# W_o's first sixteen heads loaded by a four-engine and a sixteen-engine transfer instead of one, and W_down in six transfers instead of seven

## The chip, the cores and the metric

The kernel runs on one core of one Trainium2 chip. The metric is the device time of the program in microseconds (us). Times inside the program are counted from the start of the span of the one execution that the profiler recorded; engines are named as in the profile: PE multiplies matrices (PEld loads its weights), DVE, ACT and POOL work on vectors, SP issues nearly all transfers. The core has 16 transfer engines; below, "transfer engine" always means one of these.

## What is computed

One decode step of a transformer block: two sequences, one new token each, 512 features, 32 heads of 128, a cache of 8192 keys and values for each head.

```python
x = A_x
h = x + _A_ref(_layernorm(x, axis=-1), A_k_cache, A_v_cache, A_wq, A_wo)
h2 = h + _B_ref(_layernorm(h, axis=-1), B_W_gate, B_W_up, B_W_down)
# _A_ref: softmax(q k^T / sqrt(128)) v for every head, joined, times wo (4096 x 512)
# _B_ref: (relu(x W_gate) * (x W_up)) W_down, 1376 hidden features
```

Inputs are bfloat16. Keys and values are 268 MB of the 281 MB that the program reads; the weights are the rest, W_o 4.2 MB and W_gate, W_up and W_down 1.4 MB each.

## The kernel before

The work goes in steps of four heads of one sequence: 15 such steps (the last has number Q, L53) and then two half steps of two heads, p0 and p1. For a step the keys come as one transfer of 128 partitions and the values as another (`load_tile`, L160). DVE multiplies the keys by the query (L372) and adds up the products in halves (L390, L392), PE takes a share of the scores (L339, L348), ACT makes the exponentials (L412, L430), and PE multiplies the values by them (L443). Three buffers, `bufs[0..2]`, hold keys and values in turn, and the weights of the end of the program go into the parts that are free by then: W_o into the second half of `bufs[0]` (`wo`, L125), W_gate and W_up into `bufs[2]`, W_down into `bufs[1]`.

The schedule is written out by hand. SP issues transfers in program order, and an issue waits for whatever its buffer and its completion semaphore still hold. Eight completion semaphores go round, so a transfer is issued only when the transfer eight before it has landed whole. The transfers at the end, in order: keys of p0 and p1, values of p0, W_o's heads 0 to 15 (`load_set(0)`, L559), the values of p1 in four pieces (L564), W_o's heads 16 to 23, 24 to 27 and 28 to 29 (`load_set`, L566), heads 30 and 31 (L567), W_gate and W_up in two pieces each (L578), W_down in seven pieces (L583), the output (L675). W_down's pieces are the entries of `FSETS` (L73), pairs of first row and number of 128-row chunks; the last entry, 96 rows of which are new, is loaded and used first. A transfer of W_o lays n heads as n*512 consecutive elements on each partition: 16 KB a partition for heads 0 to 15, over 128 partitions.

After p1's softmax PE multiplies W_o by the heads' outputs (L496, L503), DVE adds the residual (L614) and makes the normalised vector `hn` (L621), PE runs W_gate and W_up (L634) and then W_down chunk by chunk (L664, in the order of the pieces), DVE adds the residual (L669), and PE and DVE turn the result for the store (L673, L674).

Of the kernel before, what the change touches and what calls it, by code (L numbers as in the profile page):

```python
# [13 lines left out]
def _free(t, offset, dims):  # L14

    return bass.AP(tensor=t.tensor, offset=t.offset + offset, ap=[t.ap[0]] + [list(d) for d in dims])


def _dram(t, offset, dims):
    return bass.AP(tensor=t.tensor, offset=t.offset + offset, ap=[list(d) for d in dims])  # L20
# [3 lines left out]
def kernel(  # L24
# [13 lines left out]
    nc = tc.nc  # L38
    P = nc.NUM_PARTITIONS
    B, Sq, D = A_x.shape  # L40
    _, Hkv, Sk, Dh = A_k_cache.shape
    Hq = A_wq.shape[1] // Dh
    F = B_W_gate.shape[1]
# [23 lines left out]

    SETS = [(0, 16, 0), (16, 8, 16), (24, 4, 24), (28, 2, 28)]
    HM = 30
    SROWS = [n for _, n, _ in SETS]  # L70


    FSETS = [(0, 3), (3 * P, 3), (6 * P, 1), (7 * P, 1), (8 * P, 1), (9 * P, 1), (F - P, 1)]  # L73
    FC = 11
    AGAIN = 32

# [34 lines left out]
    hm = consts.tile([P, FC, B], bf16)  # L111
    quot = {r: consts.tile([P, Dh // r], bf16, name=f"quot{r}") for r in SROWS}
    rest = {r: consts.tile([P, r], bf16, name=f"rest{r}") for r in SROWS}
    orow = [consts.tile([P, r, B], bf16, name=f"orow{k}") for k, r in enumerate(SROWS)]
    sel = consts.tile([B, B, P // 2], bf16)
# [9 lines left out]
    wo = bufs[0][:, HALF:TILE]  # L125
# [43 lines left out]
    def ln_cols(src, dst_bkc, pfx):  # L169

        m_ps = ps.tile([P, B, KC], f32, tag="mx")
        nc.tensor.matmul(out=m_ps, lhsT=mean_w, rhs=src, start=True, stop=True)
        mean = small.tile([P, B], f32, tag=pfx + "mean")
        nc.vector.tensor_reduce(out=mean, in_=m_ps, axis=AXIS.X, op=ALU.add)
        dev = small.tile([P, B, KC], f32, tag=pfx + "dev")
        nc.vector.tensor_tensor(out=dev, in0=src, in1=_free(mean, 0, [[1, B], [0, KC]]), op=ALU.subtract)
        sq = small.tile([P, B, KC], f32, tag=pfx + "sq")
        nc.vector.tensor_tensor(out=sq, in0=dev, in1=dev, op=ALU.mult)
        v_ps = ps.tile([P, B, KC], f32, tag="mx")
        nc.tensor.matmul(out=v_ps, lhsT=mean_w, rhs=sq, start=True, stop=True)  # L180
        rstd = small.tile([P, B], f32, tag=pfx + "rstd")
        nc.vector.tensor_reduce(out=rstd, in_=v_ps, axis=AXIS.X, op=ALU.add)
        nc.scalar.activation(out=rstd, in_=rstd, func=ACT.Sqrt, bias=eps_col, scale=1.0)
        nc.vector.reciprocal(out=rstd, in_=rstd)
        nc.vector.tensor_tensor(out=dst_bkc, in0=dev, in1=_free(rstd, 0, [[1, B], [0, KC]]), op=ALU.mult)

    with tc.manual_schedule():
# [11 lines left out]
            out=nscale, in_=nscale, compare_op=ALU.not_equal, fill=-SCALE,  # L199
# [5 lines left out]
            out=ident_f, in_=ident_f, compare_op=ALU.not_equal, fill=1.0,  # L205
# [4 lines left out]
            out=sel, in_=sel, compare_op=ALU.not_equal, fill=1.0,  # L210
# [8 lines left out]
            out=pick, in_=pick, compare_op=ALU.not_equal, fill=1.0,  # L219
# [20 lines left out]
        ln_cols(xc, xn.rearrange("p c b -> p b c"), "l1")  # L240
        for r in SROWS:
            nc.vector.tensor_reduce(out=rest[r], in_=_free(ident, 0, [[1, r], [r, P // r]]), axis=AXIS.X, op=ALU.max)
# [5 lines left out]
        for g0 in range(0, NQ, 4):  # L248
            for n0 in range(NH * g0 * Dh, NH * (g0 + 4) * Dh, 4 * Dh):
                q_ps = ps2.tile([B, 4 * Dh], f32, tag="o")  # L250
                for c in range(KC):
                    nc.tensor.matmul(  # L252
                        out=q_ps, lhsT=xn[:, c, :], rhs=wq_sb[:, c, n0:n0 + 4 * Dh], start=(c == 0), stop=(c == KC - 1),
                    )
                nc.vector.tensor_copy(qrow[:, n0:n0 + 4 * Dh], q_ps)  # L255
            for b in range(B):
                r_ps = ps2.tile([P, 4, Dh], f32, tag="tp")
                for j in range(NH):
                    nc.tensor.matmul(
                        out=r_ps[j * (P // NH):(j + 1) * (P // NH)], lhsT=sel[:, b, 0:P // NH],  # L260
# [5 lines left out]
        for j in range(2):  # L266
            nc.tensor.matmul(
                out=r_ps[j * (P // 2):(j + 1) * (P // 2)], lhsT=sel[:, B - 1, :],
# [215 lines left out]
        def lay_rows(k, sps):  # L484

            r = SROWS[k]
            or_ps = ps.tile([P, B, r], f32, tag="mx")
# [4 lines left out]
        def attend_set(k, r0=0, r1=None):  # L492
            for c0 in range(r0, SROWS[k] if r1 is None else r1):
                for c in range(KC):
                    at = (SETS[k][2] + c0) * D + c * P
                    nc.tensor.matmul(  # L496
                        out=att_ps[:, c, :], lhsT=wo[:, at:at + P], rhs=orow[k][:, c0, :],
                        start=(k == 0 and c0 == 0 and c == 0), stop=False, skip_group_check=True,
                    )

        def attend(h):
            for c in range(KC):
                nc.tensor.matmul(  # L503
                    out=att_ps[:, c, :], lhsT=wo[:, h * D + c * P:h * D + (c + 1) * P], rhs=ocol[:, h, :],
                    start=False, stop=(h == Hq - 1), skip_group_check=True,
                )
# [45 lines left out]
        own_sums(Q)  # L552
        def load_set(k):
            h0, n, at = SETS[k]
            nc.sync.dma_start(
                out=wo[:, at * D:(at + n) * D], in_=_dram(A_wo, h0 * Dh * D, [[n * D, P], [1, n * D]]),
            )

        load_set(0)  # L559
        products(p0, p0.na)  # L560

# [3 lines left out]
        for k in range(1, len(SETS)):  # L565
            load_set(k)  # L566
        nc.sync.dma_start(  # L567
            out=wo[:, HM * D:Hq * D].rearrange("p (h n) -> p h n", n=D),
            in_=_dram(A_wo, HM * Dh * D, [[D, P], [Dh * D, Hq - HM], [1, D]]),
        )  # L570
# [6 lines left out]
        for w, src, c, n in ((0, B_W_gate, 0, 2), (0, B_W_gate, 2, 2), (1, B_W_up, 0, 2), (1, B_W_up, 2, 2)):  # L577
            nc.sync.dma_start(  # L578
                out=wgu[:, w, c:c + n], in_=_dram(src, c * P * F, [[F, P], [P * F, n], [1, F]]),
            )  # L580
        for f0, n in FSETS[-1:] + FSETS[:-1]:
            fc = FC - 1 if f0 == F - P else f0 // P
# [5 lines left out]
            out=z2_ps, lhsT=ones, rhs=_free(zc, ((B - 1) * NQ + groups[Q][1]) * NH, [[1, nb]]), start=True, stop=True,  # L588
# [18 lines left out]
        for k in range(1, len(SETS)):  # L607
            attend_set(k)
        for h in range(HM, Hq):
            attend(h)  # L610
# [15 lines left out]

        chunks = [(f0 + c, n) for f0, n in FSETS for c in range(n)]
        UP = 6

        def through(w_ps, k, part, cs=range(KC)):  # L630
# [18 lines left out]
            out=gate, in0=g_ps, scalar=0.0, in1=_free(rvar, 0, [[0, FC], [1, B]]), op0=ALU.max, op1=ALU.mult,  # L649
# [12 lines left out]
        for fc in order:  # L662
            for c in range(KC):
                nc.tensor.matmul(  # L664
                    out=d_ps[:, c, :], lhsT=wd_sb[:, fc, c * P:(c + 1) * P], rhs=hm[:, fc, :],
# [40 lines left out]
```

## Time and profile before

| | us |
|---|---|
| median of three runs | 661.41 (661.36 to 661.43) |
| the profiled execution | 661.18 |
| its span, first to last instruction | 659.4 |
| DVE busy | 556.6 (84%) |
| PE busy | 349.5 (53%) |
| last piece of W_down landed, in the span | 656.21 |

Transfers ran at a mean of 427 GB/s, and queue 1, which SP feeds, kept the 16 transfer engines busy for 99.0% of the span. Two other queues, called "instruction", brought 16 packets of 16 KB and six of 8 KB. The page's second part shows the span in slices, its third the queues, its fourth the chain of work that ended last. Beside these the trace has one row for each packet (start, duration, size, queue) and the moment of each step of a completion semaphore. A transfer over 128 partitions shows 16 such steps, the store of eight partitions eight together and one ahead of them, and the load of two rows of x shows two packets of data. A step is taken here as one transfer engine's end of its share. The rows do not carry the number of the transfer engine.

### The profile page before, as it was taken

What the parts mean: (1) busy time and instruction counts of PE and PEld (TensorE: products, weight loads), DVE (VectorE), ACT (ScalarE), POOL (GpSimd) and SP (SyncE); (2) the same over time, 40 slices, a digit from 0 to 9 for tenths busy, and PEclk for the clock granted to TensorE, in tenths of its full rate; (3) what the DMA queues carried; (4) which work ended last, traced back from release to release, by engine and by line L of the source; (5) the groups of instructions that cost most, each with busy time, mean ns of one, the idle gap of its engine ahead of it and who ended that gap; (6) DMA issues with size and microseconds to landing.
All of it is one profiled execution on the core that took longest, in us unless ns stands there. A gap on an engine that the chain in (4) does not pass through costs nothing.

```text
span 659.4 us, 5114 instructions
## 1 busy us (share of the span) xinstructions
PE 349.5 (53%) x2107; PEld 157.9 (24%) x2107; DVE 556.6 (84%) x250; ACT 126.6 (19%) x367; POOL 5.3 (1%) x32
## 2 busy tenths in 40 slices
PE   3530924709175380916548192753809458191886
PEld 1210311304022130402214041221403224030346
DVE  2399697989979798897969889696997979999992
ACT  1130030301103030120302102030310304200780
POOL 3000000000000000000000000000000000000000
PEclk9875875959679595966959597785957869696975
DMA  9999999999999999999999999999999999999997
GB/s 382 445 442 445 402 430 437 445 446 434 402 441 434 441 438 417 437 429 438 441 430 425 433 426 441 441 422 441 418 442 434 430 433 433 430 421 430 423 410 273
DMA packets 8458, 281.40 MB, mean 427 GB/s; under 512 B 882, under 2 KB 1780, under 8 KB 3316
## 3 DMA queue, kind: packets, MB, share of 16 engines
q1 hardware_dynamic: 8432, 281.09, 99.0%
q8 instruction: 16, 0.26, 0.2%
q14 instruction: 6, 0.05, 0.0%
q10 hardware_dynamic: 4, 0.00, 0.0%
HBM read 281.09 MB, written 0.00 MB: 426 GB/s over the span
## 4 chain that ended last, share of the span: by engine, by line
DVE 44%; DMA 36%; PE 18%; ACT 1%; issue 1%; DVEq 0%; ACTq 0%; SPq 0%
DMA tile<-in_A_k_cache_dram 31%; DVE tile L372 20%; DVE tile L390 19%; PE pv_ps L443 16%; DVE scol L392 2%; DMA tile<-in_B_W_up_dram 2%; DMA tile<-in_A_wq_dram 2%; PE q_ps L252 1%; DMA tile<-in_B_W_down_dram 1%; DVE pgq L417 1%; ACT ecol L412 1%; DVE pm L396 1%; DVE qrep L392 0%; DVE pm L407 0%; DVE hmax L409 0%
## 5 line engine op out<-in xcount | busy, mean ns | idle before, releaser
L443 PE MATMUL pv_ps<-tile,pgq 128*16 128x512 bf16 x960 | 238.5, 415 | 205.6 <-DVE pgq L417 192.9
L372 DVE TENSOR_TENSOR tile<-tile,qrep 128x28672 bf16<-128x28672 bf16 (+3 forms) x16 | 230.2, 14391 | 50.9 <-DMA tile<-in_A_k_cache_dram 50.9
L390 DVE TENSOR_TENSOR tile<-tile 128x14336 bf16<-128x14336 bf16 (+5 forms) x68 | 235.2, 3459 | 2.3
L443 PEld LDWEIGHTS <-pgq 128*16 128x16 bf16 x960 | 91.3, 96 | 347.0 <-DVE pgq L417 203.4
L349 ACT ACTIVATE tile<-t_ps 128x1024 bf16<-128x1024 bf16 x53 | 52.6, 1022 | 18.1 <-PE t_ps L348 17.5
L448 ACT ACTIVATE pv<-pv_ps 16x512 f32<-16x512 f32 (+1 forms) x16 | 9.4, 588 | 242.9 <-PE pv_ps L443 242.8
L412 ACT ACTIVATE ecol<-scol,nmax 128x256 bf16<-128x256 f32 x14 | 7.1, 507 | 193.0 <-DVE nmax L411 193.0
L339 PE MATMUL row_ps<-tile,qz 128*32 128x512 bf16 (+1 forms) x106 | 32.4, 387 | 18.8 <-ACT tile L349 18.7
L348 PE MATMUL t_ps<-ident,tile 128*128 128x128 bf16 x424 | 31.5, 225 | 5.5 <-DMA tile<-in_A_k_cache_dram 5.5
L348 PEld LDWEIGHTS <-tile 128*128 128x128 bf16 x424 | 25.1, 101 | 20.6 <-issue 14.9
L392 DVE TENSOR_REDUCE scol<-tile 128x224 f32<-128x1792 bf16 (+1 forms) x14 | 28.7, 2048 | 0.5
L307 PE MATMUL z_ps<-zc,ones 128*128 128x16 f32 (+1 forms) x8 | 2.4, 375 | 42.7 <-DVE zc L298 42.4
L378 ACT ACTIVATE tile<-tile 128x128 bf16<-128x128 bf16 x80 | 23.4, 293 | 3.5 <-DVE tile L372 3.5
L417 DVE TENSOR_TENSOR pgq<-ecol,ownb 128x1024 bf16<-128x1024 bf16 x15 | 10.4, 691 | 10.3 <-ACT ecol L412 10.3
L372 DVE TENSOR_TENSOR tile<-tile,qpair 128x5120 bf16<-128x5120 bf16 (+1 forms) x4 | 17.7, 4417 | 0.0
L339 PEld LDWEIGHTS <-qz 128*32 128x32 bf16 (+1 forms) x106 | 8.6, 93 | 28.6 <-issue 22.7
L378 ACT ACTIVATION_READ_ACCUMULATOR tile<-tile 128x1 f32 x80 | 14.9, 186 | 0.0
L252 PE MATMUL q_ps<-tile,xn 128*2 128x512 bf16 x32 | 9.1, 447 | 8.4 <-DMA tile<-in_A_wq_dram 8.4
L255 DVE CAST tile<-q_ps 2x512 bf16<-2x512 f32 x8 | 5.4, 679 | 9.7 <-PE q_ps L252 9.7
L364 ACT ACTIVATE scol<-sc_ps 32x32 f32<-32x32 f32 (+1 forms) x56 | 11.9, 213 | 7.8 <-PE sc_ps L359 7.3
L307 PEld LDWEIGHTS z_ps<-zc,ones 128*128 128x128 f32 x8 | 2.0, 310 | 43.0 <-DVE zc L298 27.6
L359 PE MATMUL sc_ps<-ident_f,tile 32*128 32x32 f32 (+1 forms) x60 | 6.4, 224 | 11.0 <-ACT tile L356 11.0
(122 smaller groups left out, 129.3 us busy)
## 6 DMA issues: line engine op xcount, KB each, us to landing
tile<-in_A_k_cache_dram SPq DMA_DIRECT2D x2, 4096.0 KB, 23.4
tile<-in_A_wq_dram SPq DMA_DIRECT2D x1, 4096.0 KB, 12.2
tile<-in_A_v_cache_dram SPq DMA_DIRECT2D x1, 4096.0 KB, 20.5
tile<-in_A_v_cache_dram SPq DMA_DIRECT2D x4, 1024.0 KB, 22.7
tile<-in_A_wo_dram SPq DMA_DIRECT2D x1, 2048.0 KB, 25.0
tile<-in_B_W_gate_dram SPq DMA_DIRECT2D x2, 688.0 KB, 13.9
tile<-in_B_W_up_dram SPq DMA_DIRECT2D x2, 688.0 KB, 12.8
tile<-in_A_wo_dram SPq DMA_DIRECT2D x1, 1024.0 KB
```

The lines of the kernel that those rows point to most:

```text
L252: nc.tensor.matmul(out=q_ps, lhsT=xn[:, c, :], rhs=wq_sb[:, c, n0:n0 + 4 * Dh], start=(c == 0), stop=(c == KC - 1),)
L339: nc.tensor.matmul(out=row_ps, lhsT=z, rhs=s.kt[:, (nv + c0 + k) * Dh:(nv + c0 + k + 4) * Dh], start=(u == 0), stop=(u == U - 1),)
L348: nc.tensor.transpose(t_ps[:, k, :], s.kt[:, t * Dh:(t + 1) * Dh], ident)
L349: nc.scalar.activation(out=s.kt[:, (nv + c0) * Dh:(nv + c0 + TPC) * Dh], in_=t_ps.rearrange("p t s -> p (t s)"), func=ACT.Copy,)
L364: nc.scalar.activation(out=scols[s.i][r, nv:s.nt].rearrange("p (u t) -> p t u", t=4), in_=sc_ps[r, :, :, j], func=ACT.Copy,)
L372: nc.vector.tensor_tensor(out=kv, in0=kv, in1=_free(s.qr, 0, [[0, n], [1, Dh]]), op=ALU.mult)
L378: nc.scalar.activation(out=kv, in_=kv, func=ACT.Copy, accum_out=scols[s.i][:, t:t + 1])
L390: nc.vector.tensor_tensor(out=lo, in0=lo, in1=hi, op=ALU.add)
L392: nc.vector.tensor_reduce(out=scol[:, s.na:s.nv], in_=_free(s.kt, s.na * Dh, [[Dh, s.nv - s.na], [1, 8]]), axis=AXIS.X, op=ALU.add,)
L412: nc.scalar.activation(out=ecol, in_=scols[s.i], func=ACT.Exp, scale=SCALE, bias=nmax, accum_out=zs[:, s.b, s.g:s.g + 1],)
L417: nc.vector.tensor_tensor(out=s.pg, in0=_free(ecol, 0, [[VG, s.nt // VG], [0, NH], [1, VG]]), in1=_free(ownb, 0, [[0, s.nt // VG], [VG, NH ...
L443: nc.tensor.matmul(out=pv_ps[s.i][r, :], lhsT=s.pg[:, u].rearrange("p j t -> p (j t)"), rhs=s.vt[:, u * VG * Dh:(u + 1) * VG * Dh], start= ...
```

## The change

Heads 0 to 15 of W_o, 2 MB in one transfer over 128 partitions, become two transfers. The first takes partitions 0 to 15 and describes the source as four blocks of four rows, so that four transfer engines carry four rows of 16 KB each. The second takes partitions 16 to 127, seven rows for each of sixteen. W_down's pieces become (4, 3, 1, 1, 1 chunks and the last 128 rows) instead of (3, 3, 1, 1, 1, 1 and the last 128 rows). The count of transfers stays the same. No instruction of another engine changes.

```diff
+    P4 = 16
+    LEVEL = 1
-    FSETS = [(0, 3), (3 * P, 3), (6 * P, 1), (7 * P, 1), (8 * P, 1), (9 * P, 1), (F - P, 1)]
+    FSETS = [(0, 4), (4 * P, 3), (7 * P, 1), (8 * P, 1), (9 * P, 1), (F - P, 1)]
...
         def load_set(k):
             h0, n, at = SETS[k]
+            w = n * D
+            if k < LEVEL:
+                nc.sync.dma_start(
+                    out=wo[0:P4, at * D:(at + n) * D],
+                    in_=_dram(A_wo, h0 * Dh * D, [[P4 // 4 * w, 4], [w, P4 // 4], [1, w]]),
+                )
+            r0 = P4 if k < LEVEL else 0
             nc.sync.dma_start(
-                out=wo[:, at * D:(at + n) * D], in_=_dram(A_wo, h0 * Dh * D, [[n * D, P], [1, n * D]]),
+                out=wo[r0:P, at * D:(at + n) * D], in_=_dram(A_wo, h0 * Dh * D + r0 * w, [[w, P - r0], [1, w]]),
             )
```

## The prediction

> **What bounds the kernel now.** I read the page first: its busy slices, its queues and its chain.
>
> ```profile
> DMA  9999999999999999999999999999999999999997
> ...
> DMA packets 8458, 281.40 MB, mean 427 GB/s; under 512 B 882, under 2 KB 1780, under 8 KB 3316
> ...
> q1 hardware_dynamic: 8432, 281.09, 99.0%
> q8 instruction: 16, 0.26, 0.2%
> q14 instruction: 6, 0.05, 0.0%
> ```
>
> The transfer engines are never idle until the last slice; queue 1 alone fills 99.0% of them. So the time is set by when the bytes have arrived plus what must follow the last byte. DVE's 44% of the chain is work under whose cover transfers run. The end of the chain in order of time says what follows:
>
> ```profile
> 638.03 12.80 DMA tile<-in_B_W_up_dram
> 650.86 0.03 issue
> 650.89 5.32 DMA tile<-in_B_W_down_dram
> 656.21 0.05 issue
> 656.26 0.28 PE d_ps L664 x4
> 656.56 0.18 DVE y L669
> ```
>
> The last chunk of W_down lands at 656.21, its four matmuls follow, and 659.4 - 656.21 = 3.2 us of tail run after it. Third, the windows over the last stage (busy of PE, PEld, DVE, ACT, POOL; then clock, share of the 16 transfer engines, GB/s):
>
> ```profile
> 652.00:653.00 1.00, 0.48 (x8) 0.41 (x6) 0.00 (x0) 0.00 (x0) 0.00 (x0) 0.50 0.94 340
> 653.00:654.00 1.00, 1.00 (x35) 1.00 (x35) 0.61 (x4) 0.00 (x0) 0.00 (x0) 0.50 0.73 268
> 654.00:655.00 1.00, 0.74 (x29) 0.68 (x27) 0.47 (x4) 0.00 (x0) 0.00 (x0) 0.50 0.50 178
> 655.00:656.00 1.00, 0.93 (x32) 0.85 (x30) 0.00 (x0) 0.00 (x0) 0.00 (x0) 0.50 0.28 95
> ```
>
> The share falls from 0.94 to 0.28 over three us: the engines do not end together, and the last ones set the end. The steps of the completion semaphores give the spread. The first load's sixteen shares land within 0.56 us, the last W_down piece's within 3.28: five within 0.32 of the first (652.93), one at 0.82, three at 1.57 to 1.82, seven at 2.89 to 3.28. The mean is 1.79, so perfectly level shares would land 1.49 us (0.23%) earlier: a ceiling for levelling.
>
> Where the lag comes from is in the packet rows. On an engine each packet begins within a few ns of the one before, so a share can be followed. The 16 KB instruction packets fall on eight engines in turn, two rounds; the first makes its engine 1.4 us late (spread 0.53 before it, 1.95 after). The 8 KB ones cost others about 0.4 each. Five engines have met none. Eight that fetch, eight that do not: the change helps if the four engines of its first transfer are among the five.
>
> **The change, part by part.** *Shares.* 16 KB packets of queue 1 take 0.613 us. Before, each engine has eight rows in this load. After, twelve have seven: -0.61 us. Four have four and seven, eleven: +1.84.
>
> *W_down's pieces.* By the trace's packets an engine's share was 8 x (2 x 0.122 + 5 x 0.046) = 3.79 us and becomes 8 x (0.159 + 0.122 + 4 x 0.046) = 3.72, and one 9 ns marker goes: -0.08 for all. The extra transfer's marker costs the four 0.01. Sum: twelve engines -0.69, four +1.77.
>
> *The end, if the four are of the five.* The twelve end at 656.21 - 0.69 = 655.52; the four at no more than 653.25 + 1.77 = 655.02. So the last piece lands at 655.52. What is late next is PE: W_down's 44 matmuls begin at 654.69, after `hm` (L659), whose own chain waits on DVE and PE. W_up's 44, with the same shapes, took 1.33 us without a wait, so W_down's cannot end before 656.02. Before, they ended at 656.54. The larger first piece (four chunks) ends 32 KB into each share, at about 652.33 + 8 x 0.159 = 653.6 on the latest engine, before it is needed. So of the 0.69 saved, 656.54 - 656.02 = 0.52 reaches the end.
>
> *Waits and queues.* The number of transfers is the same; between W_o's first load and W_down's first piece each takes the next completion semaphore. One issue of 0.33 to 0.43 us is added on SP behind values of p0. The values of p1 come behind it, but they wait for PE's reads until 611.07 anyway, 5 us later. W_o's heads 24 to 27 would now wait for the values of p0 (625.63) instead of p1's keys (615.90). The earliest engine comes to them only at 639.6, when heads 16 to 23 are done, so that costs nothing. W_down's last piece waits for a transfer landed at 649.10, no longer 650.83. Cover of the weights moved: the old load landed at 630.52 and is first read at 638.53, 8 us.
>
> *Four engines: which?* The page has no row for such a transfer. The nearest are the load of x (two rows, two data packets) and the store (eight rows, eight steps together). They bear out that few rows use few engines, not which. A weak hint: the two engines whose first packet starts first (1.77) never fetch. Bounds: the four gain nothing in lag (all of the five) or are of the seven. I take the first, since only half the engines fetch and the early starters do not.
>
> The Trainium skill ("DMA: Bandwidth & Descriptors", "Why a DMA increments its semaphore by 16 and not by 1") says that the engine count is the largest up to 16 that divides both sides' outer dimension, and that they are the lowest-numbered. By it the first transfer takes engines 0 to 3 and the second all sixteen; the trace's two and eight agree on the count, and no row here shows a number.
>
> **Rivals.**
>
> *Late four* (0.17). If the four are of the seven, the last landing is 656.21 + 1.77 = 657.98 at worst and the sum +1.8: 663.2. If one is of the middle three, 653.25 - 0.32 + 1.82 + 1.77 = 656.52, +0.3: 661.7 (0.05, in effect no change). For it: eight of sixteen engines fetch. Against it: the hint above.
>
> *Shared destinations* (0.33), the slower side. In a load of 128 partitions each engine has eight of them for itself, in this kernel always the same. With seven rows each, the second transfer's rows fall across those bounds, and two engines can write into one engine's old partitions at once. If such a pair shares the rate that one had (32 KB packets never took under 1.211 us, 27 GB/s), seven packets of 0.613 = 4.29 us become up to 8.58. Then the last landing is between 656.21 - 0.69 + 2.15 = 657.67 (half of the packets in pairs) and 659.81 (all): +1.5 to +3.6, 662.9 to 665.0, middle 664.0. It decides from 0.69 / 4.29 = 16% of the time in pairs: below that a gain is left. For it: every load of the trace has 128 partitions, so the rate seen may be a destination's and not an engine's. Against it: an 8 KB instruction packet, which goes to no tile, took 0.309 us, the same 27 GB/s, so the engine alone has that limit.
>
> The Trainium skill has a rule here: "SBUF — State Buffer", "Door 1: The DMA port swizzle", gives each port eight partitions in groups of four and 27.2 GB/s, and measures 196 GB/s for 64 partitions. Under that rule, if each engine takes seven neighbouring rows, my estimate from that section's port table is +3 to +5 us. The trace's 27 GB/s agrees with the figure and cannot say whose limit it is.
>
> *The levelling does nothing*: the extra 48 KB could be too much for its four, or W_down's end could be bound by PE at once. That is the 661.7 case above; it shares its chance.
>
> **How the numbers follow.** Forecast: the profiled execution 661.18 - 0.52 = 660.66; the median is 0.23 above that execution, so 660.9. Its own range is 660.6 (the whole 0.69 comes through) to 661.3. Chances: level 0.43, no net change 0.07, late four 0.17, shared destinations 0.33. A measurement of this kernel can tell about 0.2% (1.3 us) from no change. The level case is 0.08% and lies within, with the no-change case: 0.50. For faster by 0.2% nearly all of the ceiling would have to come through, past the PE bound: 0.02, out of the level case, whose other 0.41 counts here as no change. Late four at 1.8 (0.27%) and shared destinations are slower: 0.50, of which 0.02 is a mild collision that stays within 0.2%: so 0.02, 0.50, 0.48. The range goes from 660.6 to 665.0, the far end of the last rival; about one in ten is left out above, and little below.
>
> **What would show it.** Level: after W_o's second load the spread of a load's sixteen steps falls from 3.3 us to about 2.6, the windows' share stays above 0.9 until 654 and drops within two us, and PE's W_down matmuls run without a gap from 654.7. Late four: the spread grows to about 5. Shared destinations: 16 KB packets of queue 1 well above 0.613 us, and loads behind them landing later on engines that fetch nothing. I am wrong altogether if the chain no longer ends in W_down's transfer or if instruction packets move to other engines.

## The result, and the profile after

The changed kernel takes 670.12 us (median of four runs, 669.16 to 671.23) against 661.38 of the kernel before: 1.0133 times as long, 95% interval 1.0121 to 1.0146, 8.7 us slower. The prediction was 660.9 with a range of 660.6 to 665.0. It was wrong, on the slower side. The profiled execution after took 669.16 us with a span of 667.4, 8.0 more than the span before; the readings below are of these two.

The chain still ends in W_down's last piece. Start, duration and step:

```profile
643.68 13.49 DMA tile<-in_B_W_gate_dram
657.21 0.03 issue
657.24 6.97 DMA tile<-in_B_W_down_dram
664.20 0.05 issue
664.25 0.28 PE d_ps L673 x4
664.55 0.18 DVE y L678
```

The last piece lands at 664.20 where it landed at 656.21, and the same 3.2 us of tail follow. So the 8.0 us are all in when the bytes arrive. Where the transfers lost them shows in the windows around W_o's first load; last two columns: share of the 16 transfer engines that is busy, and GB/s. Before:

```profile
620.00:625.00 5.00, 3.62 (x17) 1.41 (x15) 4.79 (x6) 2.80 (x17) 0.00 (x0) 1.00 0.94 401
625.00:630.00 5.00, 1.93 (x6) 0.97 (x7) 5.00 (x3) 2.94 (x17) 0.00 (x0) 0.77 0.99 419
630.00:635.00 5.00, 5.00 (x15) 1.49 (x13) 5.00 (x3) 5.00 (x36) 0.00 (x0) 0.54 1.01 419
635.00:640.00 5.00, 5.00 (x76) 2.76 (x75) 4.86 (x5) 4.98 (x35) 0.00 (x0) 1.00 1.02 423
```

After:

```profile
620.00:625.00 5.00, 5.00 (x25) 2.06 (x22) 4.79 (x6) 2.63 (x19) 0.00 (x0) 1.00 0.99 306
625.00:630.00 5.00, 1.78 (x7) 0.97 (x7) 5.00 (x3) 3.12 (x17) 0.00 (x0) 0.75 0.97 206
630.00:635.00 5.00, 5.00 (x15) 1.57 (x13) 5.00 (x3) 5.00 (x36) 0.00 (x0) 0.57 1.01 210
635.00:640.00 5.00, 4.67 (x58) 2.32 (x56) 4.86 (x5) 5.00 (x36) 0.00 (x0) 1.00 0.95 293
```

The share stays near 1.0 while the rate falls to half. A busy share says only that a packet is under way on each engine. Times 5 us, the four differences are 475, 1065, 1045 and 650 KB, together 3.2 MB; at 419 GB/s that is 7.7 us, nearly the whole loss.

The packet rows say the same. W_o's 128 packets of 16 KB took 1.20 us on average (0.63 to 1.67), against 0.614 before. The trace also shows which engines carried the first transfer: its completion semaphore makes sixteen late steps, 623.18 to 630.63, where a transfer on four engines would make four (the probe run below has such a transfer). The trace gives that transfer's destination as 16 rows of 16 KB. So it ran on sixteen engines, one row each, and with the second transfer's seven every engine had eight rows as before. No engine was relieved.

### The profile page after: what moved, and what is told of

Read it like the earlier page. It is cut to its first block, busy times and chain, and to the rows that moved or that the text cites. A ratio compares the mean times of both kernels' runs of the same rounds, so it can differ in the third digit from the quotient of the medians.

```text
span 667.4 us, 5115 instructions
## 1 busy us (share of the span) xinstructions
PE 356.2 (53%) x2107; PEld 160.4 (24%) x2107; DVE 556.6 (83%) x250; ACT 126.7 (19%) x367; POOL 5.4 (1%) x32
## 4 chain that ended last, share of the span: by engine, by line
DVE 41%; DMA 40%; PE 17%; ACT 1%; issue 1%; DVEq 0%; ACTq 0%; SPq 0%
DMA tile<-in_A_k_cache_dram 30%; DVE tile L374 18%; DVE tile L392 18%; PE pv_ps L445 16%; DMA tile<-in_A_v_cache_dram 4%; DVE scol L394 2%; DMA tile<-in_B_W_gate_dram 2%; DMA tile<-in_A_wq_dram 2%; PE q_ps L254 1%; DMA tile<-in_B_W_down_dram 1%; DVE pgq L419 1%; ACT ecol L414 1%; DVE pm L398 1%; DVE qrep L394 0%; DVE pm L409 0%
## 5 line engine op out<-in xcount | busy, mean ns | idle before, releaser
L445 PE MATMUL pv_ps<-tile,pgq 128*16 128x512 bf16 x960 | 243.9, 422 | 201.2 <-DVE pgq L419 188.1
L361 PE MATMUL sc_ps<-ident_f,tile 32*128 32x32 f32 (+1 forms) x60 | 6.4, 224 | 11.1 <-ACT tile L358 11.1
## 6 DMA issues: line engine op xcount, KB each, us to landing
tile<-in_A_v_cache_dram SPq DMA_DIRECT2D x1, 4096.0 KB, 23.6
```

What stands on the lines that cost most here:

```text
L445: nc.tensor.matmul(out=pv_ps[s.i][r, :], lhsT=s.pg[:, u].rearrange("p j t -> p (j t)"), rhs=s.vt[:, u * VG * Dh:(u + 1) * VG * Dh], start= ...
```

## The experiments

Theory: *shared destinations*. Engines that write near one another share a rate, and loads over fewer than all partitions make them do so. Rivals: the added transfer and its turn of the semaphores; W_down's pieces; the order of reading at the source; a row count that is no power of two. A load of 128 partitions is called "full" below.

**W_down's pieces alone.** The kernel before with the new `FSETS` line only.

> Only W_down's pieces are changed (six, first of four chunks); W_o's first sixteen heads come by one transfer as before. Shared destinations (the whole loss comes from where the two W_o transfers write): 0.1 to 0.5 us faster than before, 660.9 to 661.3, since each engine's share of W_down is 0.08 us shorter and PE's 44 matmuls wait for one piece less. Rival, the pieces cost something (a later first chunk holds PE): 0.3 us or more slower, 661.7 or above.

661.46 us, ratio 1.0003 (0.9994 to 1.0012). No loss, and the gain of 0.1 to 0.5 did not come either. Its chain:

```profile
649.22 6.99 DMA tile<-in_B_W_down_dram
656.21 0.04 issue
656.25 0.28 PE d_ps L664 x4
```

The last piece lands at 656.21, as before, though each share should be 0.08 us shorter. The mean of its sixteen landings is 654.65 instead of 654.72, but in the two-column run below, with the same pieces, it is 654.81: single executions do not resolve 0.08 us.

**The split alone.** The new `load_set` with the old `FSETS`.

> Only W_o's load is split as in the change (16 partitions, then 112); W_down keeps seven pieces, so there is one transfer more than before. Shared destinations: about the whole loss, 669 to 671, 16 KB packets at a mean of 1.2 us. Rival, the loss needs W_down's new pieces as well: under 665.

669.10 us, 1.0122 (1.0108 to 1.0136); 16 KB packets at 1.29 us. The split is the whole loss.

**Two transfers, every row by its usual engine.**

```diff
-  16 partitions, then 112, 16 KB a row
+            for c in range(2 if k < LEVEL else 1):
+                u = w // 2 if k < LEVEL else w
+                nc.sync.dma_start(
+                    out=wo[:, at * D + c * u:at * D + (c + 1) * u],
+                    in_=_dram(A_wo, h0 * Dh * D + c * u, [[w, P], [1, u]]),
+                )
```

> W_o's first sixteen heads by two transfers of all 128 partitions, 8 KB of each row in each; W_down in six pieces. As many transfers and as many semaphore turns as in the change, but every row is written by the engine that always writes it. Shared destinations: no loss, 660.8 to 661.5, 8 KB packets at 0.31 us. Rival, an added transfer or the shifted round of completion semaphores costs the time: 665 or above.

661.30 us, 1.0002 (0.9993 to 1.0011), 8 KB packets at 0.314 us. The same number of transfers, the same turn of the semaphores and the same W_down as in the change cost nothing. In the windows the rate holds where the changed kernel has 206 and 210:

```profile
625.00:630.00 5.00, 2.00 (x9) 0.91 (x10) 5.00 (x3) 3.01 (x18) 0.00 (x0) 0.93 1.02 424
630.00:635.00 5.00, 5.00 (x19) 1.75 (x18) 5.00 (x3) 5.00 (x37) 0.00 (x0) 0.73 1.01 421
```

**Two halves of the partitions.**

```diff
+            for r0, r1 in (((0, P // 2), (P // 2, P)) if k < LEVEL else ((0, P),)):
+                nc.sync.dma_start(
+                    out=wo[r0:r1, at * D:(at + n) * D],
+                    in_=_dram(A_wo, h0 * Dh * D + r0 * w, [[w, r1 - r0], [1, w]]),
+                )
```

> W_o's first sixteen heads by two transfers of 64 partitions (0 to 63, 64 to 127), four rows for each engine in each; W_down in six pieces. Shared destinations: at any moment sixteen engines write the places of eight, so packets of 16 KB near 1.2 us and 4 to 9 us slower, 665 to 670. Rival, only a row count that is no power of two (112), or the sixteen-row transfer, is slow: within 0.5 us of before.

669.87 us, 1.0130 (1.0116 to 1.0144), 16 KB packets at 1.22 us. So neither 112 nor the sixteen-row transfer is needed for the loss. Its windows:

```profile
625.00:630.00 5.00, 1.61 (x5) 0.72 (x6) 5.00 (x3) 3.12 (x19) 0.00 (x0) 0.86 0.96 210
630.00:635.00 5.00, 5.00 (x20) 1.86 (x19) 5.00 (x3) 5.00 (x36) 0.00 (x0) 0.80 0.98 208
```

**The halves from another source.**

```diff
-                    in_=_dram(A_wo, h0 * Dh * D + r0 * w, [[w, r1 - r0], [1, w]]),
+                    in_=(_dram(A_v_cache, r0 * TILE, [[TILE, r1 - r0], [1, w]]) if k < LEVEL
+                         else _dram(A_wo, h0 * Dh * D, [[w, P], [1, w]])),
```

> The two 64-partition transfers of the halves run, but their 16 KB rows are read from the values' cache at a row pitch of 64 KB instead of from W_o (so W_o's first sixteen heads hold other data); destinations unchanged. Shared destinations: as slow as the halves run, 668 to 671, 16 KB packets near 1.2 us. Rival, the engines meet at the source, W_o's 2 MB read in another order: under 664.

668.89 us, 1.0114 (1.0094 to 1.0135), packets at 1.19 us. The source can be another tensor at another pitch and the loss stays, so it goes with the partitions that are written.

**A sixteen-row transfer added.**

```diff
+        nc.sync.dma_start(out=wo[0:16, 24 * D:32 * D], in_=_dram(A_wo, 0, [[8 * D, 16], [1, 8 * D]]))
         load_set(0)
```

> The kernel before, with one more transfer ahead of W_o's first: 16 partitions, 8 KB a row, 128 KB in all, one row for each of sixteen engines, all into partitions 0 to 15. Without any meeting it would cost 8 KB an engine, 0.31 us. Shared destinations: its packets and those that meet them in the places of four engines wait, so 0.6 to 2 us slower, 662 to 663.3. Rival, only 16 KB rows or large splits suffer: 0.3 us, 661.6.

663.02 us, 1.0027 (1.0016 to 1.0037): 1.7 us for 128 KB that would take 0.31. The full load of W_o behind it, unchanged, has 16 KB packets up to 1.25 us and a mean of 0.71 instead of 0.614. A badly placed transfer slows its neighbours in the queue too.

**Eight transfers of sixteen rows.** As the halves, with eight ranges of 16.

> W_o's first sixteen heads by eight transfers of 16 partitions, one row for each engine in each; W_down in six pieces. Shared destinations, by the four partitions that lie together: sixteen engines write four engines' places at a time, so packets of 16 KB take between 1.2 (engines spread over several transfers) and 2.4 us (all in one), and the loss is larger than the halves run's 8.6 us, 672 to 676. Rival, what is shared is a half of the partitions: as the halves run, 669 to 671.

670.94 us, 1.0146 (1.0125 to 1.0166), packets at 1.26 us. My number (672 to 676) was wrong and the rival's 669 to 671 fits. Either halves are what is shared, or the engines, up to 8 us apart in this stretch and so spread over several of the eight transfers, do not all write the same sixteen partitions. The lone loads below tell these apart.

**Loads of few rows as probes.** Three loads of 1 KB rows before W_o's first.

```diff
+        for c, r in enumerate((2, 4, 8)):
+            nc.sync.dma_start(out=wo[0:r, (24 + c) * D:(25 + c) * D], in_=_dram(A_wo, 0, [[D, r], [1, D]]))
         load_set(0)
```

> The kernel before, with three loads of 2, 4 and 8 rows of 1 KB just ahead of W_o's first load (into a place of W_o that is loaded again later). A load of few rows should show as many late completion steps as it uses engines, and when these come tells where its engines stand among the sixteen. If a four-row load uses four engines: 12 steps at issue and 4 late ones, then 8 and 8, 14 and 2. Levelling theory (the low-numbered engines are the early ones): the four late steps come within 0.5 us of the earliest engine's. Rival (they are of the fetching engines): some come 1.5 to 3.3 us later. Time: within 0.5 us of before.

One run, 661.68 us. The late steps number two, four and eight, and one more stands some 0.45 us behind each issue, whose amount the trace does not give: so few rows do use few engines. The Trainium skill ("DMA: Bandwidth & Descriptors", "Why a DMA increments its semaphore by 16 and not by 1") states the same counts. The four-row load's late steps came at 623.75, 624.31, 624.58 and 625.04; the sixteen of the values ahead of it at 622.78 to 625.74, with five by 623.51 and five from 625.33. Measured from the first of the sixteen, the four come 0.97, 1.53, 1.80 and 2.26 us later. That is not the levelling theory's number (all within 0.5 us); the rival's (some 1.5 to 3.3 us later) fits three of the four. The packet rows tell the engines apart: on an engine that the four-row load uses, a 1 KB packet follows the 4-byte marker that ends the engine's share of the values. By these rows its four engines are the fourth, ninth, tenth and eleventh of the sixteen to end the values (steps at 623.36, 624.13, 624.39 and 624.68): one of the early five, three of the middle, none of the latest five. Whether these engines had met an instruction packet was not followed.

**The four engines for real.** Partitions 0 to 15 by four transfers of four rows, then the 112 as in the change.

```diff
+                for r in range(0, P4, 4):
+                    nc.sync.dma_start(
+                        out=wo[r:r + 4, at * D:(at + n) * D],
+                        in_=_dram(A_wo, h0 * Dh * D + r * w, [[w, 4], [1, w]]),
+                    )
```

> As the change, but partitions 0 to 15 come by four transfers of four rows, which do use four engines each (the probe run showed 12 early steps and 4 late for four rows): so four engines carry eleven rows and twelve carry seven, as the change describes. Three transfers more. Levelling theory (the four are early, only the count of engines was missed): faster than the changed kernel by several us. Shared destinations: no better than the changed kernel, 669 to 674, since the 112 rows still fall across the others' places and the four engines now have three rows more.

671.22 us, 1.0146 (1.0117 to 1.0176). Each of the four transfers makes four late steps, each step 0.9 to 1.8 us (about the time of one row here) behind the same one of the transfer before. So four engines carry the sixteen rows, and with the second transfer's seven they have eleven and the other twelve have seven, as the change describes. It is no better than the change.

**Loads alone.** After the output store, when nothing else moves.

```diff
+        for r in (128, 64, 16, 4):
+            nc.sync.dma_start(out=bufs[0][0:r, 0:HALF], in_=_dram(A_v_cache, 0, [[TILE, r], [1, HALF]]))
```

> The kernel before, and after its output store four loads one after the other, alone on the transfer engines, rows of 32 KB from the values' cache into a part of a buffer that nobody reads any more: 128, 64, 16 and 4 partitions, one, one, one and one transfer. Packets of 32 KB take 1.21 us in the kernel's own loads. If four neighbouring partitions share one rate and rows are dealt to the engines in turn: 1.2, 4.8, 4.8, 4.8 us a packet. If four neighbours share it and each engine takes a block of neighbouring rows: 1.2, 2.4, 4.8, 4.8. If only the two halves of the partitions have a limit each: 1.2, 2.4, 2.4, 1.2. If nothing is shared: 1.2 in all four.

And a second kernel with partitions 16 to 127, then 0 to 31, then 0 to 7:

> As the run of lone loads, but after the store come partitions 16 to 127 (112 rows), then 0 to 31, then 0 to 7, rows of 32 KB, one load after the other. If four neighbours (and the four that stand 32 further) share one rate and each engine takes a block of neighbouring rows: 112 rows mostly 1.2 us a packet with some at 2.4, mean near 1.45, landing some 11 us after its start; 32 rows 2.4 us a packet, 4.8 us in all; 8 rows 4.8 us. If rows are dealt in turn: 112 rows near 4.8 us a packet, over 30 us in all. If 112 rows are slow for a reason of their own: 2.4 us a packet, 17 us, as in the stream.

From the first packet's start to the last completion step, rows of 32 KB (one run of each kernel):

| partitions | us | GB/s | GB/s per set (sets, see below) |
|---|---|---|---|
| 0 to 127 | 11.1 | 377 | 23.6 (16) |
| 0 to 63 | 11.4 | 185 | 23.1 (8) |
| 0 to 31 | 6.3 | 166 | 20.7 (8) |
| 0 to 15 | 5.6 | 93 | 23.2 (4) |
| 0 to 7 | 5.3 | 49 | 24.6 (2) |
| 0 to 3 | 5.4 | 24 | 24.2 (1) |
| 16 to 127 | 16.6 | 222 | |

Of the first kernel, the full load in steady flow and then the 64 partitions:

```profile
664.00:667.00 3.00, 0.00 (x0) 0.00 (x0) 0.00 (x0) 0.00 (x0) 0.00 (x0) 0.50 1.01 437
...
670.00:675.00 5.00, 0.00 (x0) 0.00 (x0) 0.00 (x0) 0.00 (x0) 0.00 (x0) 0.50 0.98 210
675.00:680.00 5.00, 0.00 (x0) 0.00 (x0) 0.00 (x0) 0.00 (x0) 0.00 (x0) 0.50 1.02 210
```

Packets took 1.213 us in the full load and 2.56 for 64 partitions in steady flow. In the loads of 16 and 4 partitions each engine has one packet, of 2.6 to 4.4 us, 3.7 and 3.2 on average where 4.8 was expected. The last completion step there comes 1.2 and 1.4 us behind the end of the last packet, against 0.3 in the full load, so the whole duration is the better measure. Start-up alone does not make these packets long: the first packets of the full load took 1.2 to 2.1 us.

Four neighbouring partitions share one rate of some 24 GB/s, start and end included. Partitions 0 to 63 run at about eight times that and not at sixteen, with 2.56 us a packet in steady flow, as 0 to 31 do: partitions 32 to 63 add nothing. Either they share the rates of 0 to 31, or each half of the partitions has a limit of its own besides. The table above counts its sets by the first, each four partitions with the four that lie 32 further; no run here loaded such a pair alone. A limit of the two halves alone is excluded: four partitions would have gone at four engines' rate. In these loads each row goes to the partition of its own number, so rows read and partitions written change together. That it is the writing is borne out by the changed kernel: packets of p0's values, a full load from another tensor, took up to 2.52 us beside the split load, and what the two have in common is the partitions that they write.

The Trainium skill ("SBUF — State Buffer", "Door 1: The DMA port swizzle") has this table: 27.6 GB/s for partitions 0 to 3, 104 for 0 to 15, 189 for 0 to 31, 196 for 0 to 63. The runs agree in shape, 24, 93, 166 and 185 here.

The 112 rows missed the number: 2.04 us a packet on average, nearly all between 1.6 and 2.3, where fair sharing with blocks of seven neighbours gave 1.45. It is neither 1.45 nor 2.4, and rows dealt in turn (4.8) are excluded. How its rows are dealt, and why all its packets slow alike, stays open.

## Why the prediction was wrong, point by point

- *The last landing plus 3.2 us.* Held: 664.20 and 667.4.
- *Shares: "twelve have seven, four have four and seven, eleven".* This step failed. The sixteen late steps of the first transfer show eight rows on every engine, so the -0.61 and +1.84 of the sum do not exist. I took the four engines from the description of the source. Four blocks of four rows that follow each other without a gap are sixteen rows, and the transfer as issued has 16 rows; that the blocks were joined on the way to the instruction is inferred from that. That the change might not do what it says stood among the rivals only as a levelling that does nothing, not as a transfer on other engines.
- *W_down: -0.08.* Not seen: 1.0003 (0.9994 to 1.0012), last landing the same; too small for these runs to show or exclude.
- *Waits and queues at nothing.* Held: the two-column run has the same round and is at 1.0002.
- *Which four?* I took four of the early five. In the probe run one of the four was of the early five and three of the middle. The latest of the four ended the values 1.06 us ahead of the last of the sixteen (624.68 and 625.74); 1.84 us more would have made it the last. That levelling would have failed even without sharing is argued from this, not shown.
- *Shared destinations (0.33).* The right mechanism, on the right grounds: all loads of the trace were full, so the 27 GB/s could be the destination's limit. The lone loads, the halves from another source and the slowed full loads show that it is. What failed is its size, +1.5 to +3.6, where the span grew by 8.0. I priced the second transfer's seven packets, all in pairs at worst, less the 0.69 saved. Per engine, the trace has 16 KB packets of 9.60 us instead of 4.91 (+4.69), 8 KB packets of 14.57 instead of 12.55 (+2.02: p1's values and W_o's heads 16 to 23), and packets of 32 KB after 600 us, 19 for each engine, at 1.266 us on average instead of 1.220 (+0.87; the slow ones start at 621.56 to 625.49: p0's values). That is +7.6, and the sixteen landings of W_down's last piece are 7.64 us later on average (662.36 instead of 654.72). The last of them is 1.84 us behind that average instead of 1.49, which adds 0.35 and makes the 8.0. So three things were short: nothing saved, eight packets at nearly double instead of seven, and 2.9 us in the full transfers before and behind, whose engines found others in their places. I had put the last term at nothing. The estimate from the Trainium skill's port table ("SBUF — State Buffer", "Door 1: The DMA port swizzle"), +3 to +5, was on the right side and short too.
- *The chances.* The trace of before could not tell a destination's limit from an engine's, and I gave the shared case less than the level one. The 8 KB instruction packet, which I held against it, shows an engine's limit of the same size and says nothing on the destination's.

No version tried beats the kernel before: the new W_down pieces alone and the two-column load are equal to it within 0.1%.

## What to carry to other kernels

Split a large load by columns, not by partitions: in every split by partitions tried here engines wrote in each other's places, at about half rate, and the transfers next to it in the queue paid too. The split by columns cost nothing. Before planning with the number of engines of a transfer, count the late steps of its completion semaphore in a trace, for the pattern written in the code need not be the one that is issued. A busy share of 1.0 does not show such sharing; the rate or the duration of one packet size does.

## What the runs showed of the hardware that was not expected

- Four neighbouring partitions took 24 GB/s though four engines wrote to them (128 KB in 5.4 us), and partitions 32 to 63 added nothing to the rate of 0 to 31 (2.56 us a packet of 32 KB in steady flow in both).
- A transfer of 128 KB over sixteen partitions cost 1.7 us in a full queue, more than five times the 0.31 us that its bytes take.
- 112 rows alone run at 222 GB/s, less than fair sharing in blocks of neighbours gives; the reason is open.
